# Norm and operand steps issued singly inside the gate's chain of MLP 1's last tile, one PSUM layout for both MLPs, and two norms in MLP 2's second group

## The chip, the cores and the metric

One NeuronCore of one Trainium2 chip runs the whole program. The metric is device microseconds of one execution, lower is better. Matrix products run on TensorE (PE in the profile, its weight loads PEld), element-wise work on VectorE (DVE), ScalarE (ACT) and GpSimd (POOL); SyncE (SP) issues the DMAs. The change leaves every result as it is and moves work in time and between engines.

## What is computed

Retention attention over 4 x 576 tokens with 8 heads of 64, then a first MLP with a gate h * cos(h), then an RMS norm and a gated second MLP, all in fp32. The change touches what follows the attention:

```python
x = _moe_ref(x=x, **moe_kwargs)          # MLP 1, 2304 tokens, 512 -> 2048 -> 512
    h = x @ w_in
    g = h * np.cos(h)
    return g @ w_out
return _moe2_ref(x=x, **moe2_kwargs)     # norm and MLP 2, 512 -> 1536 -> 512
    rms = np.sqrt(np.mean(x * x, axis=-1, keepdims=True) + 1e-06)
    xn = x / rms * rms_g
    g = xn @ w_gate
    silu = g * (1.0 / (1.0 + np.exp(-g)))
    val = xn @ w_val
    return silu * val @ w_out
```

fp32 accuracy comes from splitting each operand into a high and a low part (a cast, then a subtraction) and adding three products.

## The kernel before, in words

**MLP 1** takes the tokens in five tiles, `ORDER_A = [0, 1, 2, 4, 3]`: tiles 0, 1, 2 and 3 have 512 tokens, tile 4 has 256 and comes fourth. Each tile has 16 slices of the hidden dimension, so there are 80 steps; step i is tile i // 16, slice i % 16. The loop at L592 runs 83 times, because the second product of a step comes `LAG = 3` steps after its first. One step of the loop issues, in this order:

- `hidden` (L373): 12 matmuls of the step's hidden slice into a PSUM tile of `ps_tile` (tag g, three buffers before the change);
- on the last slice of a tile, `split_x` (L164): four casts on ScalarE and four subtractions on VectorE that make the next tile's operands;
- `gate_cos` (L379), called the chain here: a scaled copy to integers on ScalarE (L388), a reduction on VectorE (L389), the sine on ScalarE (L391), a product with the hidden slice on VectorE (L395, the last reader of the PSUM tile), the cast of the high part on ScalarE (L397, into one of LAG buffers), and the subtraction for the low part on VectorE or GpSimd (the argument `eng`, line L113). At five places `next(beside)` lets other work in; before the change that is only the conversion of MLP 2's weights, in 36 pieces (`piece_steps`), the last of them in steps 48, 51, 54 and 65 to 67;
- `out_t` of step i - 3 (L572): 12 matmuls into the four accumulators acc0 to acc3. After a tile's last slice the accumulators are copied to `xall` (L585) and the tile's norm is queued;
- `idle` (L362): pops steps of the queued norm from the list `background`. A None ends a step's popping;
- from step 67 on, `ahead(n)` (L551): the operands of MLP 2's first group (seven high and low parts and four differences, into the slots that MLP 1's weights leave) and the first two weight quads.

The norm of a tile (L307) is four squares on ScalarE with sums on VectorE, the sum's high and low part, a product with a matrix of ones on TensorE that gives the mean (L332, L333), a first guess, three Newton iterations of three VectorE steps each, and four scalings of `xall`.

**MLP 2** has three groups of 768 tokens with 12 quads each (n from 0 to 35). A quad (L687) makes seven products in the two PSUM tiles alpha and beta (tag h, two buffers, a pool of its own that opens when MLP 1's closes); between products ScalarE copies partial sums (L710), and VectorE adds, multiplies and subtracts. Eighteen matmuls of the output product (L675) are put into each quad from n = 2 on; `also(where)` lets other steps in at named places (s1, m11, r11, s4, m22, r22, m21, end). Group 2 (tokens 1536 to 2303) uses tiles 3 and 4 of MLP 1; its operands are made from n = 20 on.

**What sets the order.** From step 16 on ScalarE, VectorE and GpSimd run in the order in which the code issues (`manual_schedule`, L636); TensorE does so only in MLP 2. In MLP 1 a planner that runs when the kernel is built, with costs of its own, orders the matmuls on TensorE's queue, in general in the order of the code, but with a later product ahead of one that it takes to be not ready. Each engine's queue is strictly in order on the chip.

## Time and profile before

| | us |
|---|---|
| median of three runs | 942.12 (940.42 to 942.14) |
| profiled execution | 940.8, its span 939.0 |
| attention, and MLP 1's tile 0 beside it, to step 16 | 0 to 174.88 |
| MLP 1, tiles 0 (second half), 1 and 2, to step 48 | to 351.31 |
| MLP 1, tile 4 (256 wide), steps 48 to 63 | 351.31 to 401.46 |
| MLP 1, tile 3, steps 64 to 82 | 401.46 to 509.36 |
| MLP 2, quads 0 to 2 | 509.36 to 542.15 |
| MLP 2, the rest | 542.15 to 939.0 |

The border of two stages is the start of the first matmul of the later one. Of the 939.0 us TensorE is busy for 908.7; its busy rows overlap, so the distance from one matmul's start to the next one's is what is read here, and not their durations.

### The profile page before, as it was taken

The page shows a single profiled execution, that of the slowest core. Times are in us where ns is not written, and L with a number is a line of the kernel's source. Part 1 is how long each engine was busy: PE and PEld are TensorE (multiplying, and loading weights), DVE is VectorE, ACT ScalarE, POOL GpSimd, SP SyncE. Part 2 cuts the span into 40 slices and gives each one's busy share as a digit, 9 for nine tenths or more (in the row PEclk, how much of TensorE's full clock was granted, in tenths as well). Part 3 has the DMA queues.
Part 4 walks back from the last instruction along what each step waited for, and adds up shares of the span by engine and source line. Part 5 has one row for each costly group of instructions (what it writes and reads, how often), then busy time and mean ns, then how long its engine had stood idle before and what let it go on. Part 6 is the DMA issues. An engine that isn't in the chain of part 4 may idle for free.

```text
span 939.0 us, 12936 instructions
## 1 busy us (share of the span) xinstructions
PE 908.7 (97%) x4996; PEld 797.0 (85%) x4996; DVE 612.3 (65%) x991; ACT 462.6 (49%) x815; POOL 62.3 (7%) x58
## 2 busy tenths in 40 slices
PE   8989999999999999989898899999999999999998
PEld 7778888888887889978676899999889999999997
DVE  3999989778888886668765666676355346333332
ACT  4656666576566665564445444444422234323222
POOL 2321100000000001211221000000000000000000
PEclk9999999999999999999999999999999999999999
DMA  8956451135525433102026366667655555755531
GB/s 332 399 186 214 162 229 64 33 112 189 174 76 191 158 128 130 35 12 89 1 101 235 135 236 257 246 234 260 246 202 202 202 202 213 261 205 206 208 142 67
DMA packets 34733, 163.72 MB, mean 174 GB/s; under 512 B 4080, under 2 KB 5232, under 8 KB 23792
## 3 DMA queue, kind: packets, MB, share of 16 engines
q1 hardware_dynamic: 34672, 162.91, 47.7%
q8 instruction: 39, 0.64, 0.3%
q14 instruction: 22, 0.18, 0.1%
HBM read 123.57 MB, written 39.32 MB: 173 GB/s over the span
## 4 chain that ended last, share of the span: by engine, by line
PE 72%; DVE 18%; ACT 5%; issue 3%; DMA 1%; SPq 0%; POOL 0%; ACTq 0%; DVEq 0%; POOLq 0%
PE h L703 26%; PE acc L675 15%; PE g L176 4%; PE g L177 4%; PE g L178 4%; PE acc L177 4%; PE acc L178 4%; PE acc L176 4%; DVE w L113 2%; DVE r L395 2%; DVE r L389 2%; DVE t L131 2%; PE g L270 1%; DVE t L132 1%; ACT r L391 1%
## 5 line engine op out<-in xcount | busy, mean ns | idle before, releaser
L703 PE MATMUL h<-w 128*128 128x384 f32 x1224 | 231.1, 339 | 6.4 <-ACT s L710 3.2
L703 PEld LDWEIGHTS h<-w 128*128 128x128 f32 x1224 | 216.4, 189 | 14.2 <-ACT s L710 5.2
L675 PE MATMUL acc<-w,shi 128*128 128x512 f32 x432 | 134.4, 392 | 0.0
L176 PE MATMUL acc<-ghi,w 128*128 128x512 f32 (+1 forms) x320 | 118.2, 372 | 4.2 <-ACT ghi L397 3.1
L177 PE MATMUL acc<-glo,w 128*128 128x512 f32 (+1 forms) x320 | 118.4, 370 | 2.8 <-POOL glo L113 2.8
L176 PE MATMUL g<-xhi,w 128*128 128x512 f32 (+1 forms) x320 | 120.0, 375 | 0.7 <-ACT w L148 0.7
L178 PE MATMUL g<-xhi,w 128*128 128x512 f32 (+1 forms) x320 | 118.9, 372 | 1.2 <-DVE w L113 1.2
L177 PE MATMUL g<-xlo,w 128*128 128x512 f32 (+1 forms) x320 | 118.9, 372 | 0.0
L178 PE MATMUL acc<-ghi,w 128*128 128x512 f32 (+1 forms) x320 | 118.0, 369 | 0.0
L710 ACT COPY s<-h 128x384 f32<-128x384 f32 x108 | 51.7, 479 | 129.5 <-PE h L703 129.5
L391 ACT ACTIVATE r<-r,half_pi 128x512 f32<-128x512 f32 (+1 forms) x80 | 54.5, 681 | 79.8 <-DVE r L389 79.6
L675 PEld LDWEIGHTS acc<-w,shi 128*128 128x128 f32 x432 | 80.2, 188 | 13.4
L723 DVE TENSOR_TENSOR sg<-s,h 128x384 f32<-128x384 f32 x54 | 29.9, 554 | 93.1 <-PE h L703 52.6
L675 PE MATMUL acc<-w,slo 128*128 128x512 f32 x216 | 85.4, 396 | 0.0
L176 PEld LDWEIGHTS acc<-ghi,w 128*128 128x128 f32 x320 | 60.3, 189 | 15.7 <-ACT ghi L397 4.3
L177 PEld LDWEIGHTS acc<-glo,w 128*128 128x128 f32 x320 | 60.4, 189 | 13.9 <-POOL glo L113 4.3
L397 ACT CAST ghi<-r 128x512 fp32r<-128x512 f32 (+1 forms) x80 | 46.2, 578 | 50.8 <-DVE r L395 47.6
L735 ACT CAST shi<-v 128x384 fp32r<-128x384 f32 x72 | 37.1, 515 | 69.0 <-DVE v L731 68.9
L176 PEld LDWEIGHTS g<-xhi,w 128*128 128x128 f32 x320 | 61.1, 191 | 11.6 <-ACT w L148 0.9
L178 PEld LDWEIGHTS g<-xhi,w 128*128 128x128 f32 x320 | 60.9, 190 | 11.8 <-DVE w L113 1.6
L177 PEld LDWEIGHTS g<-xlo,w 128*128 128x128 f32 x320 | 61.1, 191 | 10.1
L178 PEld LDWEIGHTS acc<-ghi,w 128*128 128x128 f32 x320 | 60.4, 189 | 9.9
(86 smaller groups left out, 1300.0 us busy)
## 6 DMA issues: line engine op xcount, KB each, us to landing
w<-s SPq DMA_DIRECT2D x24, 1024.0 KB, 4.8
raw<-w_dram SPq DMA_DIRECT2D x36, 512.0 KB, 4.0
w<-w SPq DMA_DIRECT2D x18, 1024.0 KB, 5.1
w<-s SPq DMA_DIRECT2D x24, 768.0 KB, 6.3
raw<-w_dram SPq DMA_DIRECT2D x16, 1024.0 KB, 7.4
x<-qkv_dram SPq DMA_DIRECT2D x15, 1024.0 KB, 9.0
s<-w SPq DMA_DIRECT2D x12, 1024.0 KB, 4.8
s<-w SPq DMA_DIRECT2D x12, 768.0 KB, 3.9
```

The source lines that it names most:

```text
L113: eng.tensor_tensor(dst, src, hi.bitcast(F32), op=ALU.subtract)
L131: nc.vector.scalar_tensor_tensor(t, high, -2 ** 30, t, op0=ALU.bitwise_and, op1=ALU.bitwise_or)
L176: nc.tensor.matmul(dst, a[0], b[0], start=start, stop=False)
L177: nc.tensor.matmul(dst, a[0], b[1], start=False, stop=False)
L178: nc.tensor.matmul(dst, a[1], b[0], start=False, stop=stop)
L391: nc.scalar.activation(r, r, AF.Sin, bias=half_pi, scale=1.0)
L397: nc.scalar.copy(hi, r)
L675: nc.tensor.matmul(acc, (hi, hi, lo)[k][:, c], w[:, u, (0, 1, 0)[k], :], start=start and u == 0 and k == 0, stop=stop and u == 1 and k == 2)
L703: nc.tensor.matmul(bank, a[:, wp], xp[:, c], start=start and kc == 0 and n == 0, stop=kc == 1 and n == 2, skip_group_check=True)
L710: nc.scalar.copy(t, alpha)
L723: nc.vector.tensor_tensor(t, s, bank, op=ALU.add)
L735: nc.scalar.copy(hi, t)
```

## The change

- `norm` returns a list of single steps, each with its engine's letter (A, D or P), and the low part of the sum goes to VectorE. A sum's square and add are now two steps. Between low, mean and guess stand two None each.
- Outside the last tile a step of the loop pops up to two norm steps instead of one: `idle()` and then one more if its letter is D in an odd step and A in an even one. In tile 4 popping stops as before once tile 1's norm is done.
- In the last tile (steps 64 to 79), where no weight piece is due, the five places inside the chain each take one step: A between copy and sine, D between reduction and product, A, D and D behind. They come from `ready` (operands and first quads, filled by `ahead`) and else from `background` (tile 2's norm). In steps 80 to 82 six more places follow.
- The chain's last subtraction goes to VectorE in all steps from 48 on.
- PSUM: acc0 to acc3 live in one pool for the whole kernel; from step 8 on the attention's four banks become h (two buffers), acc4 and acc5, and MLP 1's hidden slices and means take these four in turn.
- The norms of tiles 4 and 3 run in MLP 2's second group, at m22 (up to five A or D steps) and end (up to five) of its quads 1 to 10 (n = 13 to 22). The copies of the last tile's accumulators are spread over quads 0 and 1.

Step by step, the lists give this order. Tile 0's norm starts at step 18 as before; its guess and first Newton step come at step 29, two VectorE steps come at steps 31, 33, 35 and 37. Tile 1's guess comes at step 49 and its two-step visits are at steps 49, 51, 53, 55 and 57, its one-step visits at 50, 52, 54 and 56; tile 2's first square follows at 58. Tile 2's low part comes at step 72, its mean at 74, its guess in the chain of step 77, its last eleven VectorE steps in steps 80 to 82. In the second group the half-wide norm of tile 4 is in n = 13 to 15, that of tile 3 in n = 16 to 18.

```diff
-    banks1 = ExitStack()
-    psp = banks1.enter_context(tc.tile_pool(name="psp", bufs=1, space=PSUM, reuse_waits="tile"))
+    psp = pool("psp", 1, space=PSUM)
+    att = ExitStack()
+    psa = att.enter_context(tc.tile_pool(name="psa", bufs=1, space=PSUM, reuse_waits="tile"))
+    late = {}
     dram = pool("dram", 1, space=bass.MemoryType.DRAM)
+    taken = [0]
+    def hidden_tile():
+        return late["psh"].tile([P, 512], F32, tag="h", bufs=2, name="h")
+    def acc_tile(m):
+        return (psp if m < KC else late["psh"]).tile([P, 512], F32, tag=f"acc{m}", name="acc")
     def ps_tile():
-        return psp.tile([P, 512], F32, tag="g", bufs=3, name="g")
-    def acc_tile(m):
-        return psp.tile([P, 512], F32, tag=f"acc{m}", name="acc")
+        if "psh" not in late:
+            return psa.tile([P, 512], F32, tag="g", bufs=3, name="g")
+        taken[0] += 1
+        return hidden_tile() if taken[0] % 2 else acc_tile(KC + taken[0] // 2 % 2)
...
+    ready, background, normal = [], [], []
...
-            if kc == 0:
-                st["s"] = q
-            else:
-                nc.vector.tensor_tensor(st["s"][:, :n], q[:, :n], st["s"][:, :n], op=ALU.add)
-        def total():
-            hi, lo = tmp(F32R), tmp(F32R)
-            s = st["s"][:, :n]
-            nc.scalar.copy(hi[:, :n], s)
-            minus(nc.gpsimd, lo[:, :n], hi[:, :n], s)
-            st["parts"] = hi, lo
+        def add(kc):
+            nc.vector.tensor_tensor(st[0][:, :n], st[kc][:, :n], st[0][:, :n], op=ALU.add)
+        def high():
+            st["parts"] = tmp(F32R), tmp(F32R)
+            nc.scalar.copy(st["parts"][0][:, :n], st[0][:, :n])
+        def low():
+            hi, lo = st["parts"]
+            minus(nc.vector, lo[:, :n], hi[:, :n], st[0][:, :n])
         def mean():
-            st["mean"] = late["mean"]() if "mean" in late else ps_tile()
+            st["mean"] = hidden_tile() if t in ORDER_A[-2:] else ps_tile()
             hi, lo = st["parts"]
             nc.tensor.matmul(st["mean"][:, :n], ones_r, hi[:, :n], start=True, stop=False)
             nc.tensor.matmul(st["mean"][:, :n], ones_r, lo[:, :n], start=False, stop=True)
...
             nc.vector.scalar_tensor_tensor(x(kc), x(kc), rg_sb[:, kc:kc + 1], st["y"],
                                            op0=ALU.mult, op1=ALU.mult)
-        background.extend([lambda kc=kc: square(kc) for kc in range(KC)])
-        background.append(total)
-        background.extend([None, mean, None, guess] if t != ORDER_A[-1] else [None, mean, guess])
-        background.extend([lambda s=s: newton(s) for _ in range(3) for s in range(3)])
-        background.extend([lambda kc=kc: scale(kc) for kc in range(KC)])
-        background.append(lambda: normal.append(t))
-    def idle(count=1):
+        steps = [("A", lambda: square(0))]
+        for kc in range(1, KC):
+            steps += [("A", lambda kc=kc: square(kc)), ("D", lambda kc=kc: add(kc))]
+        steps += [("A", high), ("D", low), None, None, ("P", mean), None, None, ("D", guess)]
+        if t in ORDER_A[-2:]:
+            steps = [step for k, step in enumerate(steps) if step or k == steps.index(None)]
+        steps += [("D", lambda s=s: newton(s)) for _ in range(3) for s in range(3)]
+        steps += [("D", lambda kc=kc: scale(kc)) for kc in range(KC)]
+        steps.append(("D", lambda: normal.append(t)))
+        return steps
+    def idle(count=1, engines="ADP"):
         for _ in range(count):
             if background and not background[0]:
                 background.pop(0)
                 break
-            if background:
-                background.pop(0)()
+            if background and background[0][0] in engines:
+                background.pop(0)[1]()
+    def pull(engine):
+        for steps in (ready, background):
+            if steps and steps[0] and steps[0][0] == engine:
+                steps.pop(0)[1]()
+                return
+    def other_steps():
+        for engine in "ADADD":
+            pull(engine)
+            yield
     g_parts = {}
...
             late["steps"] = operand_steps(0)
-        while late["steps"] and (len(slots) == n or late["steps"][0].__name__ != "high"):
-            late["steps"].pop(0)()
-        if 7 <= n < 11:
+        if n < 7:
+            places.append(slot())
+            ready.append(late["steps"].pop(0))
+            while late["steps"] and late["steps"][0][0] != "A":
+                ready.append(late["steps"].pop(0))
+        elif n < 11:
             slot()
             if n % 2 == 0:
                 a, b = (t.rearrange("p a b c -> p (a b c)") for t in slots[-2:])
                 sides.append((a[:, :6 * 2 * P].rearrange("p (h n c) -> p h n c", h=2, n=3),
                               b.rearrange("p (h n c) -> p h n c", h=2, n=4)))
-                for step in quad_steps(len(sides) - 1).values():
-                    for part in step:
-                        part()
-        elif n >= 11:
+                for steps in quad_steps(len(sides) - 1).values():
+                    ready.extend(steps)
...
             t0 = TILES[t][0]
-            for m in range(KC):
-                nc.scalar.copy(xall[:, m, t0:t0 + n], accs[t][m][:, :n])
-            norm(t)
+            copies = [lambda m=m: nc.scalar.copy(xall[:, m, t0:t0 + n], accs[t][m][:, :n]) for m in range(KC)]
+            if t == ORDER_A[-1]:
+                late["copies"] = copies
+            else:
+                for copy in copies:
+                    copy()
+            if t not in ORDER_A[-2:]:
+                background.extend(norm(t))
...
+            late["psh"] = pool("psh", 1, space=PSUM)
...
-                     nc.vector if i < NF1 or begun(i) is not None else nc.gpsimd,
-                     piece_steps(begun(i), max(valued, default=None)))
+                     nc.vector if i < NF1 or i >= 3 * NF1 or begun(i) is not None else nc.gpsimd,
+                     piece_steps(begun(i), max(valued, default=None)) if begun(i) is not None or valued
+                     else other_steps() if i >= LAST - NF1 else iter(range(5)))
+        elif i >= LAST:
+            for engine in "ADADDD":
+                pull(engine)
         if i >= LAG:
             out_t(*steps[i - LAG])
         if more:
...
+            idle()
+            idle(1, "D" if i % 2 else "A")
+        elif i >= LAST - NF1:
+            idle(1, "P")
         if i >= LAST - NF1 + LAG and len(slots) < NSLOT_A:
             ahead(len(slots))
         if i == MANUAL - 1:
...
+        alpha = hidden_tile()[:, :HALF]
+        beta = hidden_tile()[:, :HALF]
         plain, sums = side(q)
...
-            assert len(normal) == (4, 5)[g]
+            assert len(normal) == (3, 5)[g]
...
+        if n < 2:
+            for where in ("s4", "end"):
+                more[where] = more.get(where, []) + [("A", late["copies"].pop(0))]
+        if n == NQUAD:
+            background.extend(norm(ORDER_A[-2]) + norm(ORDER_A[-1]))
         if g == 1 and 0 < q < NQUAD - 1:
-            more["end"] = more.get("end", []) + [lambda: idle(4)]
+            more["m22"] = more.get("m22", []) + [("D", lambda: idle(5, "AD"))]
+            more["end"] = more.get("end", []) + [("D", lambda: idle(5))]
         quad(g, q, fill, more)
```

## Rows read from the trace of the kernel before

**Rows 1.** Two stretches: us; busy PE, PEld, DVE, ACT, POOL; clock, DMA share, GB/s.
```profile
401.46:509.36 107.90, 98.02 (x426) 78.88 (x425) 76.68 (x115) 53.03 (x90) 21.80 (x16) 0.97 0.24 91
509.36:542.15 32.79, 29.12 (x145) 26.63 (x144) 17.92 (x33) 17.10 (x33) 0.00 (x0) 0.95 0.30 112
```

**Rows 2.** TensorE's waits from 401.46 to 509.36: total us, times, longest us.
```profile
PE g L332 <- ACT nt L325: 3.6, 2, 3.3
PE acc L176 <- ACT ghi L397: 3.1, 2, 1.7
PE acc L177 <- POOL glo L113: 2.8, 4, 0.9
```

**Rows 3.** Timeline of TensorE: first matmuls of steps 37, 47, 53 and 63.
```profile
291.01 0.39 PE L176 MATMUL g<-xhi,w 128*128 128x512 f32 x1
...
345.41 0.39 PE L176 MATMUL g<-xhi,w 128*128 128x512 f32 x1
...
369.78 0.28 PE L176 MATMUL g<-xhi,w 128*128 128x256 f32 x1
...
398.58 0.28 PE L176 MATMUL g<-xhi,w 128*128 128x256 f32 x1
```

**Rows 4.** Timeline of TensorE around steps 66 to 68; in brackets the idle time before.
```profile
417.49 0.79 PE L332 MATMUL g<-nt,ones_r 128*128 128x512 f32 x1 [3.33 <-ACT nt L325]
...
422.39 0.39 PE L176 MATMUL g<-xhi,w 128*128 128x512 f32 x1
...
423.52 0.39 PE L176 MATMUL acc<-ghi,w 128*128 128x512 f32 x1
```

**Rows 5.** Timeline of the other engines: a chain, then VectorE's operand steps, tile 3.
```profile
404.86 0.69 ACT L388 ACTIVATE r<-g,quarter 128x512 int32<-128x512 f32 x1
407.06 0.69 DVE L395 TENSOR_TENSOR r<-g,r 128x512 f32<-128x512 f32 x1 [0.79 <-ACT r L391]
407.84 0.62 ACT L397 CAST ghi<-r 128x512 fp32r<-128x512 f32 x1 [0.81 <-DVE r L395]
...
457.92 1.63 POOL L113 TENSOR_TENSOR glo<-r,ghi 128x512 fp32r<-128x512 f32 x1 [5.22 <-ACT ghi L397]
458.56 1.81 DVE L113 TENSOR_TENSOR w<-xall,w 128x768 fp32r<-128x768 f32 x1 [0.16 <-ACT w L533]
...
465.30 0.95 DVE L113 TENSOR_TENSOR w<-xall,w 128x768 fp32r<-128x768 f32 x1
```

**Rows 6.** Timeline of VectorE in tile 4, and its split for tile 3.
```profile
374.17 0.42 DVE L389 SCALAR_TENSOR_TENSOR r<-r,g 128x256 f32<-128x256 int32 x1 [0.30 <-ACT r L388]
375.16 0.42 DVE L395 TENSOR_TENSOR r<-g,r 128x256 f32<-128x256 f32 x1 [0.58 <-ACT r L391]
...
376.49 0.42 DVE L389 SCALAR_TENSOR_TENSOR r<-r,g 128x256 f32<-128x256 int32 x1 [0.30 <-ACT r L388]
...
377.86 0.42 DVE L395 TENSOR_TENSOR r<-g,r 128x256 f32<-128x256 f32 x1
378.80 0.43 DVE L113 TENSOR_TENSOR glo<-r,ghi 128x256 fp32r<-128x256 f32 x1 [0.53 <-ACT ghi L397]
379.14 0.69 DVE L131 SCALAR_TENSOR_TENSOR t<-raw,t 128x512 int32<-128x512 int32 x1
...
380.58 0.68 DVE L347 SCALAR_TENSOR_TENSOR nt<-nt 128x512 f32<-128x512 f32 x1
381.18 0.42 DVE L389 SCALAR_TENSOR_TENSOR r<-r,g 128x256 f32<-128x256 int32 x1
...
400.38 2.68 DVE L113 TENSOR_TENSOR xlo<-xall,xhi 128x512 fp32r<-128x512 f32 x4 [0.39 <-ACT xhi L170]
```

**Rows 7.** TensorE's only wait from 131 to 371.
```profile
PE acc L176 <- ACT xall L585: 1.1, 1, 1.1
```

**Rows 8.** Timeline of TensorE in MLP 2's second group: its two longest waits.
```profile
673.25 3.42 PE L703 MATMUL h<-w 128*128 128x384 f32 x18 [1.42 <-ACT s L710]
...
699.36 2.35 PE L703 MATMUL h<-w 128*128 128x384 f32 x12 [0.96 <-DVE sg L723]
```

More of the change, by code (lines that the diff above doesn't have):

```diff
@@ L186, in proj @@
             mm3(dst[:, :n], (whi[:, c], wlo[:, c]), (xhi[:, :n], xlo[:, :n]), kc == 0, kc == KC - 1)
-    att = ExitStack()
     ap = att.enter_context(tc.tile_pool(name="ap", bufs=2, reuse_waits="tile"))
@@ L251, in values @@
             if c == 0:
-                total[0] = psp.tile([P, NPAIR, P], F32, tag="st", name="total")
+                total[0] = psa.tile([P, NPAIR, P], F32, tag="st", name="total")
             for p in range(NPAIR):
@@ L301, in body @@
     nc.sync.dma_start(rg_sb, rg)
-    background, normal = [], []
-    late = {}
+    ready, background, normal = [], [], []
     def norm(t):
@@ L314, in square @@
         def square(kc):
-            q = tmp()
+            q = st[kc] = tmp()
             nc.scalar.activation(q[:, :n], x(kc), AF.Square)
-            if kc == 0:
-                st["s"] = q
-            else:
-                nc.vector.tensor_tensor(st["s"][:, :n], q[:, :n], st["s"][:, :n], op=ALU.add)
-        def total():
-            hi, lo = tmp(F32R), tmp(F32R)
-            s = st["s"][:, :n]
-            nc.scalar.copy(hi[:, :n], s)
-            minus(nc.gpsimd, lo[:, :n], hi[:, :n], s)
-            st["parts"] = hi, lo
+        def add(kc):
[6 more added lines that the diff above has]
+            minus(nc.vector, lo[:, :n], hi[:, :n], st[0][:, :n])
         def mean():
-            st["mean"] = late["mean"]() if "mean" in late else ps_tile()
+            st["mean"] = hidden_tile() if t in ORDER_A[-2:] else ps_tile()
             hi, lo = st["parts"]
@@ L386, in gate_cos @@
         k, r, hi, lo = k[:, :n], r[:, :n], hi[:, :n], lo[:, :n]
-        beside = beside or iter(range(5))
         nc.scalar.activation(k, ps, AF.Identity, bias=quarter, scale=INV_2PI)
@@ L506, in keep @@
                 fetch_values(q + 2)
-        return {"r11": [high0, low0], "m22": [sums0], "r22": [high1], "m21": [low1], "end": [keep]}
+        return {"r11": [("A", high0), ("D", low0)], "m22": [("D", sums0)], "r22": [("A", high1)],
+                "m21": [("D", low1)], "end": [("D", keep)]}
     kept = [[dram.tile([P, 2, n, 2 * P], F32, tag=f"s{n}_{q}", name=f"s{n}_{q}") for n in (3, 4)] for q in range(NQUAD)]
@@ L525, in place @@
         def place(k):
-            t = places.pop(0) if g else slot()
+            t = places.pop(0)
             ops[g, k] = t, t[:, 0, :, :HALF], t[:, 1, :, :HALF]
@@ L537, in low @@
                 minus(nc.vector, lo, hi, src)
-            return [high, low]
+            return [("A", high), ("D", low)]
         def difference(dst, a, b):
-            return [lambda: nc.vector.tensor_tensor(dst, a, b, op=ALU.subtract)]
+            return [("D", lambda: nc.vector.tensor_tensor(dst, a, b, op=ALU.subtract))]
         t1 = difference(x(0, 0), x(0, 1), x(0, 0))
@@ L583, in out_t @@
             t0 = TILES[t][0]
-            for m in range(KC):
-                nc.scalar.copy(xall[:, m, t0:t0 + n], accs[t][m][:, :n])
-            norm(t)
+            copies = [lambda m=m: nc.scalar.copy(xall[:, m, t0:t0 + n], accs[t][m][:, :n]) for m in range(KC)]
+            if t == ORDER_A[-1]:
+                late["copies"] = copies
+            else:
+                for copy in copies:
+                    copy()
+            if t not in ORDER_A[-2:]:
+                background.extend(norm(t))
     steps = [(t, f) for t in ORDER_A for f in range(NF1)]
@@ L624, in body @@
                 converted[0] += 1
-        if i // NF1 != 3 or 1 not in normal:
-            idle(3 if i >= LAST - NF1 else 1)
+        if i < LAST - NF1 and (i // NF1 != 3 or 1 not in normal):
+            idle()
+            idle(1, "D" if i % 2 else "A")
+        elif i >= LAST - NF1:
+            idle(1, "P")
         if i >= LAST - NF1 + LAG and len(slots) < NSLOT_A:
@@ L647, in body @@
     order.enter_context(tc.manual_schedule(engines=ENGINES | {mybir.EngineType.PE}))
-    banks1.close()
-    psp = pool("psp2", 1, space=PSUM)
-    def hidden_tile():
-        return psp.tile([P, 512], F32, tag="h", bufs=2, name="h")[:, :HALF]
-    late["mean"] = lambda: psp.tile([P, 512], F32, tag="h", bufs=2, name="h")
     bx = pool("bx", 2)
@@ L659, in body @@
     gp = pool("gp", 2)
+    assert not ready and not places and not background
     places.extend(bx.tile([P, 2, 2, HALF], F32R, tag="b", name="b") for _ in range(2))
@@ L689, in also @@
         def also(where):
-            for step in more.get(where, ()):
+            for _, step in more.get(where, ()):
                 step()
         val = q % 2
-        alpha = hidden_tile()
-        beta = hidden_tile()
+        alpha = hidden_tile()[:, :HALF]
+        beta = hidden_tile()[:, :HALF]
         plain, sums = side(q)
```

## The prediction

> **What bounds the kernel now.** First the stages, by the first matmul of each: MLP 1's last tile, steps 64 to 82, takes 107.90, TensorE is busy for 98.0 of it and its granted clock is 0.97 [rows 1]. Next, who keeps TensorE waiting there: the high part of a norm's sum (3.6 in two waits), the high part of a gate (3.1), and the low part that GpSimd makes (2.8) [rows 2]; no transfer. So this stage is set by the element-wise chain, the others nearly all by TensorE. Then what the stage would take in full flow. Where nothing waits, step 47 starts 54.40 after step 37, so a step of 24 wide matmuls is 5.44; steps 53 to 63 are 28.80 for ten, 2.88 for a half-wide one [rows 3]. One product is thus 2.72 wide and 1.44 narrow. The stage has 16 wide hidden products (43.5), 3 narrow and 16 wide output products (4.3 + 43.5) and, after the change, one mean of two matmuls (2 x 5.44/24 = 0.45): 91.8. It now takes 16.1 more. The waits named are 9.5 of that; the rest is what comes behind a wait, a pipeline that fills again and a clock that has fallen: 3% of 107.90 is 3.2. The wait of 3.33 before the mean of tile 2 [rows 4] is the longest.
>
> **The last tile: -16.1.** Without guests the chain needs 2.98 from its first copy to the cast (404.86 to 407.84), with ScalarE idle for 0.79 and 0.81 in it, waiting for VectorE [rows 5]. After the change the A steps fall into this idle time, and VectorE has three operations of 0.69 of its own and up to three guests. The widest guest, 768 elements, took 0.95 at 465.30 and 1.81 at 458.56, where GpSimd ran beside it from 457.92 [rows 5]. GpSimd has nothing left from step 48 on, so I take 0.95: 3 x 0.69 + 3 x 0.95 = 4.92 for a step in which TensorE needs 5.44. The chain keeps up, the mean of tile 2 comes two steps behind its low part, and the waits of [rows 2] go: 107.90 becomes 91.8.
>
> The Trainium skill, "SBUF — State Buffer", section "Who interferes with whom", says that a VectorE instruction with two SBUF inputs contends with a GpSimd instruction that reads SBUF. Here the trace agrees, 1.81 against 0.95. By that rule alone the subtraction's move would be a gain in tile 4 too, the term for tile 4 below would be nothing and the sum about -10; the rows of tile 4 speak against it.
>
> **A PSUM slot held by the mean: +2.5.** Slices and means take four slots in turn, so the mean of step 74 has the slot that step 78 wants. It is free when the guess has read it, and the guess is the last guest of chain 77. That chain starts when hidden 77 ends, and takes 2.98 to the cast, 0.62 for it, 0.69 for the subtraction and 0.69 for the guess's first operation: 5.0, and 0.6 more if guests hold it up. TensorE has one output product, 2.72, until it wants the slot: a wait of 2.3 to 2.9. If the planner puts the next output product ahead, the wait is nothing. Bounds 0 and 3.0.
>
> **Tile 4: +4.2.** Its chain now takes 2.32 a step (374.17 to 376.49), under TensorE's 2.88, because VectorE does a norm step while ScalarE casts and GpSimd subtracts [rows 6]. With the subtraction on VectorE the norm steps queue behind it, and the next chain behind them: reduction to product 0.99 (374.17 to 375.16), product to subtraction 0.94 (377.86 to 378.80), 0.34 to what follows (379.14), and 0.60 for each norm step (380.58 to 381.18): 2.27 bare, 2.87 with one, 3.47 with two. Against 2.32 the steps 51 to 57 add 0.60 (second norm step), 0.55, 1.15, 0 (a weight piece, VectorE subtracts there before too), 1.15, 0.55 and 1.15: 5.15. Step 50 adds some 0.5, and tile 2's square on ScalarE at 58 as much: 6.2. Steps 59 to 62 cost the same before and after, so this is not made up in comparison. The split of tile 3 queues behind chain 62 on both engines; its first subtraction ended 0.67 after 400.38, hidden 64 started at 401.46, so 0.4 is spare: hidden 64 starts 5.8 late. Meanwhile TensorE could do two narrow output products, 2.9, if the planner has them ahead; it does such things, since at 422.39 hidden 68 starts before the output product at 423.52 [rows 4]. Bounds 2.9 and 5.8; I take the middle. **Clock: +0.7.** The 3.2 of clock above came in two falls, each behind waits; a gap of this length may bring one, 1.6, or none.
>
> **Accumulator copies: +0.6 and +0.5.** TensorE's only wait in tiles 1 and 2, 1.1, is for the copies at step 34, behind a chain that VectorE delays [rows 7]. One more Newton step (0.60) is ahead of them, at step 33. Bounds 0 and 1.2. At step 66 tile 4's copies come behind a chain that needs more than the 4.16 of a wide and a narrow product. No row shows it; between nothing and twice the row above (2.2), with another hidden product as cover, I take 0.5.
>
> **MLP 2's second group: +1.7.** Two norms in place of most of one. Before, the square, sum and cast at the end of n = 13 made TensorE wait 1.42, and four Newton steps at the end of n = 15 0.96 [rows 8]: of 4 x 0.69 some 1.8 were free. After: half-wide operations at n = 13, -0.4. At n = 15 ten half-wide steps (0.43 each, [rows 6]): five at m22 push VectorE back by about 1.3, five at the end are 2.15: 1.65 beyond the free 1.8, against 0.96: +0.7. At n = 17 guess and three Newton steps, 3.2, are 1.4 beyond it, against 0.2: +1.2. Tile 4's mean, 0.2. Bounds 0 (m22 fits into VectorE's own waits) and 3.
>
> **Quads 0 to 2: 0.** Three squares ahead of the first partial sum go (about -0.5); two accumulator copies stand ahead of the first copy of quads 1 and 2 (up to +0.5 each). The stretch has a clock of 0.95, 5% of 32.79 = 1.6, which may come again or not [rows 1]. Bounds -2 and +1.
>
> **At nothing.** The eleven VectorE steps of steps 80 to 82 (about 0.65 each, 7.2) end some 12.3 after hidden 79, with chain 79 ahead of them; VectorE is wanted in quad 0 after four output products and two quad products, about 13. If that 0.7 is gone, it costs one for one. The DMAs of the first two quads are issued two steps later on SyncE, and are wanted in quad 1, over 12 later. The fourth buffer brings nothing: no wait for a PSUM slot stands in [rows 2, 7]. The attention's banks change hands at step 8, after the last attention read or up to 1 before it. In tiles 1 and 2 the second norm step in odd steps is hidden by the lag of three steps.
>
> **Sum.** -16.1 + 2.5 + 4.2 + 0.7 + 0.6 + 0.5 + 1.7 + 0 = -5.9. The profiled execution, 940.8 with its span of 939.0, becomes 934.9; the median of the runs is 1.3 above it: 942.1 - 5.9 = 936.2.
>
> **The rivals.** (1) The planner hides what it can: the slot wait, the clock's fall and the copies at step 66 are nothing and tile 4 costs 2.9: -16.1 + 2.9 + 0.6 + 1.7 = -10.9, 931.2. For it: the order in [rows 4]. Against it: the same planner put a mean where TensorE waited 3.33. (2) TensorE runs in the code's order, and the upper bounds hold: 3.0 + 5.8 + 1.6 + 0.6 + 2.2 + 1.7 = 14.9, so -1.2 and 940.9, no difference that can be told. For it: the regular 5.44 and 2.88 of [rows 3] are the code's order. (3) Slower: the guests hold up the chain that they sit in. A cast into a slot waits until TensorE has read the weights that lay there, and it now stands ahead of the sine. The spare of a step is 5.44 - 4.92 = 0.52; when A steps wait longer than that, or the 768-wide steps take over 1.12 (at 1.81 a step is 7.5), the waits for gate parts in [rows 2] stay and only the norm's 3.6 with one fall of the clock, 1.6, go: -5.2 + 10.2 of the terms above = +5.0, 947.1. Against it: the slots are filled two steps after their last reader, if TensorE keeps the code's order.
>
> **How the numbers follow.** Forecast 48%, its own range 932.5 to 940; rival 1 24%; rival 2 15%; rival 3 10%; others 3%. The range 930.0 to 942.0 takes in the forecast, most of rival 1 and of rival 2. A measurement of this kernel can tell about 0.2% from no change, 1.9 us. Faster by more: 48 + 24 + a third of rival 2, 77%. Within: 13%. Slower: 10%.
>
> **What would show it.** In the trace after: the stage from the first matmul of step 64 to that of quad 0, near 95 (92 and a wait before hidden 78 of about 2.5); no wait for the sum's high part or for GpSimd; a wait for the split's low part before hidden 64 of 3 to 6, with the reductions of tile 4 about 2.9 and 3.5 apart; a wait of TensorE near 1.7 in n = 16 and 1.4 in n = 18. It is wrong if steps 69 to 79 are further apart than 5.44, or if tile 4's narrow steps stay at 2.88 to the end.

## The result and the profile after

The changed kernel takes 930.97 us (median of five runs, 929.44 to 936.03) against 942.14 of before: a ratio of 0.9894, 95% interval 0.9861 to 0.9927. It is faster by 11.2, where the forecast said 5.9; the time lies within the range of the forecast. The profiled execution took 929.44, the fastest of the five, with a span of 927.7.

Stage by stage, by the same first matmuls as before (step 16, 48, 64, quads 0, 3, 13 and 19):

| stage | before | after | difference | forecast |
|---|---|---|---|---|
| start to step 16 | 174.88 | 173.36 | -1.5 | 0 |
| steps 16 to 47 | 176.43 | 176.41 | 0.0 | +0.6 |
| tile 4, steps 48 to 63 | 50.15 | 56.29 | +6.1 | together -8.2 |
| tile 3, step 64 to quad 0 | 107.90 | 90.43 | -17.5 | |
| quads 0 to 2 | 32.79 | 33.79 | +1.0 | 0 |
| quads 3 to 12 | 115.90 | 115.97 | +0.1 | 0 |
| quads 13 to 18 | 73.21 | 73.56 | +0.4 | +1.7 |
| quad 19 to the end | 207.74 | 207.84 | +0.1 | 0 |

Three stages of the kernel after, as in [rows 1] (us; busy PE, PEld, DVE, ACT, POOL with counts; clock; DMA share, GB/s): tile 4, tile 3, quads 0 to 2.

```profile
349.77:406.06 56.29, 54.15 (x402) 51.13 (x401) 37.35 (x81) 27.89 (x62) 1.30 (x1) 1.00 0.23 71
406.06:496.49 90.43, 90.43 (x408) 74.58 (x406) 67.23 (x107) 50.62 (x83) 0.00 (x0) 1.00 0.27 101
496.49:530.28 33.79, 28.02 (x145) 25.01 (x144) 21.19 (x38) 16.86 (x32) 0.00 (x0) 1.00 0.34 128
```

In the last tile TensorE is busy for 90.43 of 90.43: every wait of [rows 2] is gone from this stretch, and so are the falls of the clock that came behind them. It is even 1.4 shorter than the 91.8 of full flow, one narrow product, because the planner put output products of tile 4 ahead of hidden 64. That border is therefore no fair one, and below the two tiles are read together: 158.05 before, 146.72 after. Where an experiment moves products over the border of quad 0, the stretch is taken to quad 3: 190.84 before, 180.51 after.

How it became so stands in the queues of ScalarE and VectorE in the last tile after (start, duration, engine, line, operation, in brackets the idle time before it and what ended it).

```profile
432.16 0.68 ACT L413 ACTIVATE r<-acc,quarter 128x512 int32<-128x512 f32 x1
432.74 0.82 ACT L559 CAST w<-xall 128x768 fp32r<-128x768 f32 x1
433.61 0.72 ACT L416 ACTIVATE r<-r,half_pi 128x512 f32<-128x512 f32 x1
...
432.90 0.68 DVE L414 SCALAR_TENSOR_TENSOR r<-r,acc 128x512 f32<-128x512 int32 x1
433.60 0.96 DVE L123 TENSOR_TENSOR w<-xall,w 128x768 fp32r<-128x768 f32 x1
434.48 0.68 DVE L420 TENSOR_TENSOR r<-acc,r 128x512 f32<-128x512 f32 x1
```

Between two operations of the chain (L413 to L420) stands one guest on each engine. The 768-wide guest of VectorE takes 0.96, the value that the forecast chose between 0.95 and 1.81 [rows 5]; GpSimd has nothing to do.

Tile 4 pays. VectorE there, as in [rows 6], and then TensorE's waits in this stage, where before it had none.

```profile
372.41 0.41 DVE L414 SCALAR_TENSOR_TENSOR r<-r,h 128x256 f32<-128x256 int32 x1
...
374.35 0.43 DVE L123 TENSOR_TENSOR glo<-r,ghi 128x256 fp32r<-128x256 f32 x1 [0.53 <-ACT ghi L422]
374.69 0.68 DVE L356 SCALAR_TENSOR_TENSOR nt<-nt 128x512 f32<-128x512 f32 x1
375.29 0.41 DVE L414 SCALAR_TENSOR_TENSOR r<-r,acc 128x256 f32<-128x256 int32 x1
...
377.58 0.69 DVE L358 SCALAR_TENSOR_TENSOR nt<-nt 128x512 f32<-128x512 f32 x1
378.30 0.69 DVE L354 TENSOR_TENSOR nt<-nt 128x512 f32<-128x512 f32 x1
378.91 0.42 DVE L414 SCALAR_TENSOR_TENSOR r<-r,h 128x256 f32<-128x256 int32 x1
```

```profile
365.18 0.39 PE L186 MATMUL acc<-ghi,w 128*128 128x256 f32 x1 [0.90 <-ACT xall L612]
...
403.04 0.74 PE L186 MATMUL acc<-ghi,w 128*128 128x256 f32 x4 [0.29 <-ACT ghi L422]
405.36 0.74 PE L186 MATMUL acc<-ghi,w 128*128 128x256 f32 x4 [0.62 <-ACT ghi L422]
```

The norm steps (L354 to L358) now stand behind the subtraction (L123) and ahead of the next reduction (L414). With one norm step between them two reductions are 2.88 apart (372.41 to 375.29), with two 3.62 (375.29 to 378.91); the forecast had 2.87 and 3.47. The wait at 365.18 is new and no step of the forecast has it: it is for the copies of tile 2's accumulators at step 50.

The second price stands in quad 0: TensorE's 2.09 for VectorE, which first had to finish tile 2's norm.

```profile
496.49 3.31 PE L738 MATMUL h<-w 128*128 128x384 f32 x18
501.89 2.36 PE L738 MATMUL h<-w 128*128 128x384 f32 x12 [2.09 <-DVE sg L758]
...
498.63 2.74 DVE L361 SCALAR_TENSOR_TENSOR xall<-xall,rg_sb,nt 128x512 f32<-128x512 f32 x4
501.29 0.55 DVE L758 TENSOR_TENSOR sg<-s,h 128x384 f32<-128x384 f32 x1
```

In MLP 2's second group TensorE waits in three quads, as in [rows 8].

```profile
660.76 3.41 PE L738 MATMUL h<-w 128*128 128x384 f32 x18 [0.72 <-ACT s L745]
686.63 2.35 PE L738 MATMUL h<-w 128*128 128x384 f32 x12 [1.34 <-DVE sg L758]
711.36 2.35 PE L738 MATMUL h<-w 128*128 128x384 f32 x12 [0.74 <-DVE sg L758]
```

### The profile page after: what moved, and what is told of

Its sections match the earlier page's. It is cut to its first block, busy times and chain, and to the rows that moved or that the text cites. A ratio compares the mean times of both kernels' runs of the same rounds, so it can differ in the third digit from the quotient of the medians.

```text
span 927.7 us, 12893 instructions
## 1 busy us (share of the span) xinstructions
PE 900.8 (97%) x4996; PEld 790.4 (85%) x4996; DVE 619.5 (67%) x1022; ACT 461.9 (50%) x815; POOL 28.5 (3%) x27
## 4 chain that ended last, share of the span: by engine, by line
PE 76%; DVE 16%; ACT 5%; issue 2%; DMA 1%; SPq 0%; ACTq 0%; DVEq 0%
PE h L738 27%; PE acc L710 15%; PE acc L186 8%; PE acc L187 7%; PE acc L188 7%; PE h L187 3%; PE h L188 3%; PE h L186 3%; DVE t L141 1%; DVE r L420 1%; DVE t L142 1%; DVE w L123 1%; DVE r L414 1%; DVE s L251 1%; DVE glo L123 1%
## 5 line engine op out<-in xcount | busy, mean ns | idle before, releaser
L123 DVE TENSOR_TENSOR glo<-r,ghi 128x512 fp32r<-128x512 f32 (+1 forms) x78 | 49.8, 639 | 33.2 <-ACT ghi L422 31.3
L765 DVE TENSOR_TENSOR v<-s,h 128x384 f32<-128x384 f32 x54 | 29.8, 552 | 53.5 <-PE h L738 40.9
L123 DVE TENSOR_TENSOR slo<-v,shi 128x384 fp32r<-128x384 f32 x72 | 40.1, 557 | 36.7 <-ACT shi L770 36.7
L738 PE MATMUL h<-b,w 128*128 128x384 f32 x288 | 56.7, 337 | 0.0
L187 PE MATMUL h<-xlo,w 128*128 128x512 f32 (+1 forms) x148 | 54.3, 367 | 0.1
L188 PE MATMUL h<-xhi,w 128*128 128x512 f32 (+1 forms) x148 | 54.2, 366 | 0.0
```

Source lines behind the costliest of these rows:

```text
L123: eng.tensor_tensor(dst, src, hi.bitcast(F32), op=ALU.subtract)
L187: nc.tensor.matmul(dst, a[0], b[1], start=False, stop=False)
L188: nc.tensor.matmul(dst, a[1], b[0], start=False, stop=stop)
L738: nc.tensor.matmul(bank, a[:, wp], xp[:, c], start=start and kc == 0 and n == 0, stop=kc == 1 and n == 2, skip_group_check=True)
L765: nc.vector.tensor_tensor(t, s, bank, op=ALU.add)
```

## The experiments

Three questions: which part brings the gain (the smaller load, the spreading, or the place inside the chain); what tile 4's loss is made of; and where the waits in quad 0 and in group 2 come from. Each ratio is to runs of the kernel before on the same chip, with its 95% interval.

### Which part brings the gain

**Only the subtraction to VectorE**, in the kernel before, from tile 4 on.

```diff
-                     nc.vector if i < NF1 or begun(i) is not None else nc.gpsimd,
+                     nc.vector if i < NF1 or i >= 3 * NF1 or begun(i) is not None else nc.gpsimd,
```

> The kernel before with one part of the change alone, the chain's last subtraction on VectorE in all steps from 48 on. Theory: what held up the last tile was mostly the bursts of norm and operand steps, GpSimd's subtraction only the 2.8 of TensorE's waits for it; and in tile 4 VectorE is now full at 2.87 a step against TensorE's 2.88, so the chain does not catch up there and hidden 64 waits 2 to 3 for the split. Tiles 4 and 3 together stay within 2 of the 158.1 before. Rival: GpSimd is the main cause, with its slower subtraction and the contention: tiles 4 and 3 take 6 or more less.

Measured: 948.83, ratio 1.0068 (1.0048 to 1.0088), slower. Tile 4 takes 53.48, 3.3 more than before; both tiles 165.97, 7.9 more. The waits of TensorE in them (in all, times, longest):

```profile
PE acc L176 <- ACT ghi L397: 7.5, 3, 4.6
PE g L332 <- ACT nt L325: 6.3, 1, 6.3
```

The waits for the gate's low part on GpSimd are gone, those for the two high parts together have more than doubled: with bursts left in VectorE's queue, one more operation in it makes each of them later. Neither the theory nor its rival had this. A part of the 7.9 is TensorE's clock, which fell more often among these waits, to a mean of 0.91 in the last tile against 0.97 in [rows 1]:

```profile
403.81:516.30 112.49, 98.75 (x410) 79.46 (x408) 79.54 (x131) 53.79 (x92) 2.02 (x2) 0.91 0.24 90
```

**Only tile 4's norm to the second group**, in the kernel before, eight steps at the end of each quad.

```diff
...
-            norm(t)
+            if t != ORDER_A[-2]:
+                norm(t)
...
+        if n == NQUAD:
+            norm(ORDER_A[-2])
...
-            more["end"] = more.get("end", []) + [lambda: idle(4)]
+            more["end"] = more.get("end", []) + [lambda: idle(8)]
```

> The kernel before with another part alone: the norm of tile 4 leaves the last tile and runs in MLP 2's second group, at the end of its quads, up to eight steps at a time. Theory: half of the last tile's loss comes from that norm, which stands beside the operand steps from step 72 on: the waits from 460 to 475 go, tiles 4 and 3 together take 6 to 8 less than 158.1, and the second group pays some 5 more, since eight steps in one place hold up the next quad: 939 to 941 in all. Rival: the operand steps alone hold the chain up; tiles 4 and 3 gain no more than 2, and the kernel is slower than before by 3 or more.

Measured: 949.24, ratio 1.0074 (1.005 to 1.0097), slower. The two tiles gain 2.9 (155.19) where 6 to 8 were expected, the wait for the norm of tile 2 is the same 3.33 as in [rows 4], and quads 13 to 18 lose 10.2 (83.43), in these waits and two falls of the clock behind the first two:

```profile
690.35 3.92 PE L704 MATMUL h<-w 128*128 128x384 f32 x12 [3.33 <-DVE v L731]
706.70 3.50 PE L704 MATMUL h<-w 128*128 128x384 f32 x12 [3.01 <-DVE sg L724]
733.48 2.37 PE L704 MATMUL h<-w 128*128 128x384 f32 x12 [1.27 <-DVE sg L724]
```

Up to ten steps in two places of a quad (the kernel after) cost 0.35 there, eight in one place 10.2, the two falls of the clock included. The steps are not quite the same: in the kernel before a square and its sum are one step, and the norm's low part is GpSimd's.

**The changed kernel with nothing spread in the last tile**: three norm steps at the end of a step, and whatever a step has ready in one go.

```diff
-                     else other_steps() if i >= LAST - NF1 else iter(range(5)))
-        elif i >= LAST:
-            for engine in "ADADDD":
-                pull(engine)
+                     else iter(range(5)))
...
-            idle(1, "P")
+            idle(3)
...
+            while ready:
+                ready.pop(0)[1]()
```

> The changed kernel, but in the last tile nothing is spread: the norm takes three steps at the end of each step, and what a step has ready (slices and quads 0 and 1) is issued in one go behind the step's last matmul, as before the change. Theory A (the gain is the spreading): waits for the gate's and the norm's high parts come back in the last tile, which takes 97 to 104 instead of 90.4; step 48 to quad 0 154 to 160, 938 to 944. Theory B (the gain is that the low parts left GpSimd and tile 4's norm the stage): last tile 90 to 92, 931. Neither part alone gained, so a sum between them (934) would say that they work together.

Measured: 939.32, ratio 0.9962 (0.9945 to 0.9978). To quad 0 it is 141.25, which looks like a gain, but the planner had started quad 0 ahead of three output products: to quad 3 it is 188.66, 8.1 more than after and 2.2 less than before. The largest wait, and what VectorE and ScalarE did ahead of it:

```profile
494.56 0.51 PE L737 MATMUL h<-w 128*128 128x384 f32 x2
499.87 0.79 PE L186 MATMUL acc<-ghi,w 128*128 128x512 f32 x1 [4.80 <-ACT ghi L422]
...
494.63 0.43 DVE L515 TENSOR_TENSOR z<-z 128x256 f32<-128x256 f32 x1
...
495.09 1.14 ACT L521 CAST w<-z 128x512 fp32r<-128x512 f32 x2 [2.74 <-DVE z L515]
496.13 0.68 ACT L413 ACTIVATE r<-acc,quarter 128x512 int32<-128x512 f32 x1
```

ScalarE stood for 2.74 at a cast of quad 1's weights that needed VectorE's sums, with the start of chain 78 behind it. The expected length to quad 0 was a miss, the total was met; spreading is worth 8.1 of the 10.3 that the stretch gained. In these 8.1 stands a fall of the clock that began in the wait:

```profile
497.80:504.60 6.80, 4.73 (x10) 3.43 (x11) 3.37 (x5) 3.51 (x6) 0.00 (x0) 0.50 1.01 401
```

**Spread, but behind the chain**: the same five steps per step, pulled after the chain has been issued instead of between its operations.

```diff
-                     else other_steps() if i >= LAST - NF1 else iter(range(5)))
+                     else iter(range(5)))
+            if i >= LAST - NF1 and begun(i) is None and i != LAST - NF1 + 4:
+                for engine in "ADADD":
+                    pull(engine)
```

> The changed kernel, with the same single steps in the last tile in the same steps, but all five behind the chain and none inside it. Theory A: what helps is that each step has few of them and that tile 4's norm is gone, and a lag of three steps covers the rest: steps 69 to 71 become some 6.2 apart on VectorE for three steps, 2.3 in all against a slack of 11, and TensorE does not wait: within 1 of the changed kernel. Theory B: the place inside the chain is what helps, since guests behind it make each step longer than 5.44; the waits for gate parts come back and the stage of tile 3 takes 5 to 10 more.

Measured: 930.04, ratio 0.9867 (0.985 to 0.9884); to quad 3 180.32, against 180.51. That the guests fill the chain's idle time [rows 5] is not what brings the gain; few of them in each step is.

**GpSimd in the last tile again**, VectorE in tile 4 as in the change.

```diff
-                     nc.vector if i < NF1 or i >= 3 * NF1 or begun(i) is not None else nc.gpsimd,
+                     nc.vector if i < NF1 or (i // NF1 == 3) or begun(i) is not None else nc.gpsimd,
```

> The changed kernel, with the chain's last subtraction in the last tile (from step 64, but not in the steps with a weight piece) on GpSimd as before the change. Theory: the slack of three steps covers it, GpSimd's 1.3 to 1.6 instead of 0.69 makes the parts later but not more than 5.44 apart: tiles 4 and 3 together within 1 of 146.7. Rival: beside GpSimd the 768-wide guests take 1.8 instead of 0.95 and a step with three of them 7.5; the waits for gate parts come back, 4 or more.

Measured: 929.72, ratio 0.9869 (0.9848 to 0.989); both tiles 146.60, against 146.72. In the last tile the engine of the subtraction makes no difference, though [rows 2] name GpSimd for 2.8: with only the subtraction moved, above, such waits had come back as waits for the cast. Behind the tile it does make one: to quad 3 it is 179.23, 1.3 less than after, as VectorE, with fewer operations in its queue, is done sooner and the wait of 2.09 in quad 0 shrinks.

```profile
503.96 2.38 PE L738 MATMUL h<-w 128*128 128x384 f32 x12 [0.63 <-DVE sg L758]
```

### What tile 4's loss is made of

**GpSimd in tile 4**, with the change's two norm steps in odd steps.

```diff
-                     nc.vector if i < NF1 or i >= 3 * NF1 or begun(i) is not None else nc.gpsimd,
+                     nc.vector if i < NF1 or i >= LAST - NF1 or begun(i) is not None else nc.gpsimd,
```

> The changed kernel, with the chain's last subtraction in tile 4 (steps 48 to 63) back on GpSimd, on VectorE only from step 64. Theory: tile 4 loses its 4 us because the norm steps queue behind that subtraction (reductions 2.9 to 3.5 apart); with GpSimd a step with two norm steps is 0.99 + 0.34 + 2 x 0.60 = 2.5, under TensorE's 2.88, so the chain of step 62 is over 4 earlier, hidden 64 starts without a wait, and tiles 4 and 3 together take 3 to 4 less than the 146.7 of the changed kernel: 927 for the time. Rival: it is the second norm step in odd steps alone, on whichever engine the subtraction is: no more than 1 less.

Measured: 932.51, ratio 0.9897 (0.9878 to 0.9917). Both tiles 145.95, 0.8 less than after: a miss, as the engine alone is not tile 4's loss. Chain 62's reduction does start 50.3 after hidden 48 instead of 53.6, but then no output product is put ahead of hidden 64 (192 matmuls of output products start in tile 4's stage, 209 after), and TensorE waits for the split of tile 3 that queues behind the chain:

```profile
405.42 0.50 PE L186 MATMUL h<-xhi,w 128*128 128x512 f32 x1 [1.29 <-ACT xhi L180]
406.32 0.51 PE L187 MATMUL h<-xlo,w 128*128 128x512 f32 x1 [0.40 <-DVE xlo L123]
```

**The guess of tile 2 two steps earlier**: no empty steps between its mean and its guess.

```diff
-        steps += [("A", high), ("D", low), None, None, ("P", mean), None, None, ("D", guess)]
+        steps += [("A", high), ("D", low), None, None, ("P", mean)] + ([None, None] if t != ORDER_A[2] else []) + [("D", guess)]
```

> The changed kernel, without the two None between the mean and the guess of tile 2, so that the guess comes in the chain of step 75 and not of step 77. Theory: the wait of 2.09 in quad 0 for VectorE comes from the norm steps left over to steps 80 to 82, and these are late because hidden 78 waits for the PSUM slot of the mean; now step 78 follows step 77 after 5.44, seven steps instead of eleven are left over, and the wait in quad 0 goes: 2 less, 929. Rival: the first quads of MLP 2 wait anyway, for the partial sums and the table of the new activation; quads 0 to 2 stay within 0.5 of the 33.8 of the changed kernel.

Measured: 931.16, ratio 0.9875 (0.9858 to 0.9893). The wait of 2.09 in quad 0 is gone, and hidden 78 starts 5.44 after hidden 77 instead of 8.29. The stage of quads 0 to 2 gained only 1.0 (32.74), as its profile holds a fall of the clock:

```profile
498.97:531.71 32.74, 29.23 (x145) 26.36 (x144) 16.54 (x31) 16.74 (x32) 0.00 (x0) 0.95 0.34 127
519.80:523.20 3.40, 3.34 (x12) 2.83 (x11) 2.25 (x5) 1.38 (x3) 0.00 (x0) 0.50 0.28 113
```

**Both together**, the early guess and GpSimd in tile 4.

> Both edits, the subtraction of tile 4 on GpSimd and the early guess. Theory: the two losses are apart and add: 5 to 6 less than the changed kernel, 925. Rival: one of them only covers the other, 3 less.

Measured: 929.28, ratio 0.9855 (0.9837 to 0.9873); both tiles 145.66, quads 0 to 2 31.65 without a fall. So the late guess cost 33.79 - 31.65 = 2.1, in quad 0; to quad 3 both edits save 3.2 (177.31), where 5 to 6 were expected. The late guess acts in two ways. The mean keeps its PSUM slot, so hidden 78 comes late (at 480.00 in the profile of after, when the guess, 0.69 from 479.25, has read the mean), and VectorE stands idle ahead of chain 78's reduction for 3.47, against 0.91 with the early guess alone (first after, then the early guess):

```profile
483.87 0.69 DVE L414 SCALAR_TENSOR_TENSOR r<-r,acc 128x512 f32<-128x512 int32 x1 [3.47 <-ACT r L413]
```

```profile
483.63 0.69 DVE L414 SCALAR_TENSOR_TENSOR r<-r,acc 128x512 f32<-128x512 int32 x1 [0.91 <-ACT r L413]
```

And four more of the norm's steps are left over for the time behind that chain, some 0.72 each. Either is worth more than the wait of 2.09, and no run separates the two.

**Both, and one norm step a step in tile 4.**

```diff
             idle()
-            idle(1, "D" if i % 2 else "A")
+            if i < 3 * NF1:
+                idle(1, "D" if i % 2 else "A")
```

> The changed kernel with the early guess, the subtraction of tile 4 on GpSimd, and one norm step a step in tile 4 instead of up to two. Theory: the norm steps were the other half of tile 4's loss; the reductions are 2.32 apart again, hidden 64 starts without a wait, and tiles 4 and 3 together come to 143 to 143.5, quads 0 to 2 to 31.7: 926.5 for the time. Rival: hidden 64 waits in any case for the split that stands behind chain 62: 145.5, no gain over the kernel with both edits alone.

Measured: 927.09, ratio 0.9848 (0.9824 to 0.9871). Both tiles 143.04, where full flow by the forecast's unit prices is 141.7: three steps with a narrow and a wide product (4.16 each), thirteen narrow ones (2.88), and the last tile's 91.8. The reductions are now 2.32 to 2.33 apart, under TensorE's 2.88, as before the change in [rows 6]:

```profile
384.46 0.42 DVE L414 SCALAR_TENSOR_TENSOR r<-r,acc 128x256 f32<-128x256 int32 x1 [0.31 <-ACT r L413]
...
386.79 0.42 DVE L414 SCALAR_TENSOR_TENSOR r<-r,h 128x256 f32<-128x256 int32 x1 [0.30 <-ACT r L413]
```

**The early guess and one norm step a step, with the subtraction on VectorE**: the diffs of the early guess and of the one norm step.

> Tile 4 has one norm step a step instead of two, the guess of tile 2 comes early, and the low part is still VectorE's. Theory A (the second norm step and the subtraction each carry about half of tile 4's loss): bare chain 2.27 plus one norm step 0.60 is 2.87 against TensorE's 2.88, so nothing builds up in the steps, only what has built up before; step 48 to quad 0 145 to 146, against 146.45 with two norm steps on VectorE and 143.04 with one norm step and GpSimd. Theory B (only the number of norm steps counts, the engine doesn't): 143 to 143.5 as with GpSimd. Theory C (only the engine counts): 146.5. Quads 0 to 2 31.7, and 1.6 more if the clock falls.

Measured: 930.44, ratio 0.9862 (0.9839 to 0.9884). Both tiles 144.59: both the second norm step and the engine count, the norm step somewhat more than expected. Where no weight piece stands between them, the reductions of steps 52 to 59 are 2.88 to 2.89 apart, TensorE's own period:

```profile
385.37 0.41 DVE L414 SCALAR_TENSOR_TENSOR r<-r,acc 128x256 f32<-128x256 int32 x1
...
388.26 0.41 DVE L414 SCALAR_TENSOR_TENSOR r<-r,h 128x256 f32<-128x256 int32 x1
```

A chain that is late when tile 4 begins stays late; with GpSimd it catches up 0.55 in each step. From 146.45 (two norm steps, VectorE) the second norm step takes 1.9 off, GpSimd 0.8, both 3.4.

**Three PSUM buffers instead of four**, with the early guess.

```diff
-        return hidden_tile() if taken[0] % 2 else acc_tile(KC + taken[0] // 2 % 2)
+        return hidden_tile() if taken[0] % 3 else acc_tile(KC)
```

> The kernel with the early guess, with three PSUM buffers in the rotation of slices and means instead of four. Theory A (the fourth buffer brings nothing, as no wait of the kernel before was for a slot): step 48 to quad 0 146.5 and 931, no difference. Theory B (the mean holds one of three slots from its matmuls until the guess has read it, so that only two are left for hidden products): a wait of 1 to 3 at each of the two means of the last tile, step 48 to quad 0 148 to 152, 933 to 937.

Measured: 932.99, ratio 0.9888 (0.986 to 0.9915), which the times alone can't tell from the 0.9875 with four. The trace can: steps 16 to 47 take 1.7 more (178.04), both tiles 2.3 more (148.79), and TensorE waits in tile 4 for the product on VectorE, the last reader of a slot, for 3.0 and 0.9:

```profile
PE h L186 <- DVE r L420: 3.0, 4, 1.2
...
PE acc L186 <- DVE r L420: 0.9, 2, 0.5
```

From step 16 to quad 0 no wait of before was for a slot, with three buffers; the change makes chains late, and the fourth buffer takes up this lateness. At the means of the last tile, where the expectation that it is needed had put its waits, there is none (90.08).

### The second group

**The fastest so far, with the two norms spread over three places of the quads**, one to five steps at each by a table.

```diff
+SPREAD = {0: {"end": 3}, 1: {"r11": 2, "end": 2}, 2: {"r11": 2, "m22": 1, "end": 5}, 3: {"r11": 1, "m22": 1, "end": 2},
+          4: {"r11": 5, "m22": 5, "end": 5}, 5: {"r11": 1, "m22": 1, "end": 2}, 6: {"r11": 4, "m22": 4, "end": 5}, 7: {"m22": 1}}
...
-            more["m22"] = more.get("m22", []) + [("D", lambda: idle(5, "AD"))]
-            more["end"] = more.get("end", []) + [("D", lambda: idle(5))]
+            for where, count in SPREAD[q].items():
+                more[where] = more.get(where, []) + [("D", lambda count=count, where=where: idle(count, "ADP" if where == "end" else "AD"))]
```

> The fastest so far (early guess, GpSimd in tile 4, one norm step a step there), with the two norms of the second group spread over three places of each quad product by a table instead of five at one and five at another. Theory A (the waits of the group, 0.72, 1.34 and 0.74, come from ten VectorE steps in a row ahead of the quad product's own work): quads 13 to 18 go from 73.57 to 70.5 to 72, 924 to 925.5. Theory B (the work of VectorE in these quads is the bound wherever it stands, or the waits are for the norm's own chain): 73.5, 927.

Measured: 923.98 (922.54 to 924.72), ratio 0.9797 (0.9773 to 0.982), the fastest of all. Quads 13 to 18 take 70.45, and TensorE is busy for 70.36 of it:

```profile
404.19:496.71 92.52, 92.26 (x424) 76.71 (x423) 69.24 (x109) 50.65 (x82) 0.74 (x1) 1.00 0.27 99
644.25:714.70 70.45, 70.36 (x365) 64.83 (x364) 40.91 (x78) 26.30 (x56) 0.00 (x0) 1.00 0.61 221
```

All three waits of the group are gone. Its work on VectorE is no bound; where it stands is.

## Why the prediction was right, and short by half

**The last tile, -16.1: right.** 91.8 was forecast without any carry from tile 4. Where tile 4 costs almost nothing, the stage took 92.5 (the early guess with one norm step on GpSimd, and the spread group): 15.4 less than before, and of the missing 0.7 a wait of 0.26 for the accumulator copies at step 66 is one part, which the forecast had at 0.5. The reason given beside it, that guests fit into the chain's idle time, was not the one that counts: behind the chain they cost the same. What the forecast called 4.92 of VectorE in a step of 5.44 leaves room at both places. The forecast also misread one of its rows: the 0.79 of [rows 5] is VectorE's idle time, waiting for the sine, and not ScalarE's; ScalarE's own two there are 0.76 ahead of the sine (at 406.30) and 0.81 ahead of the cast.

**Tile 4, +4.2: right, by the mechanism and nearly the size.** The middle of its bounds, 2.9 and 5.8, is 4.35 and not 4.2. The two tiles' 146.72 less 50.15 for tile 4 before and 91.8 for the last tile is 4.8, where tile 4 and the copies at step 66 were forecast at 4.7. Chain 62's reduction starts 53.6 after hidden 48, against 46.6 before, 7.0 later where 6.2 was forecast; the planner gave back part of it with products put ahead, so that no wait of 3 to 6 stands ahead of hidden 64, which was to be the sign, but 0.29 and 0.62 ahead of output products. Taking the second norm step and VectorE's subtraction away is worth 3.4 of 146.45. The forecast missed the wait of 0.90 at step 50 within it: it took the second norm step in tiles 1 and 2 to be hidden by the lag of three steps, which is so for the output products, but the copies at a tile's end come behind the chain too.

**The rule of the Trainium skill, "SBUF — State Buffer", "Who interferes with whom"**, would have made the move of the subtraction a gain in tile 4. The contention is there (with GpSimd kept in tile 4 a scaling took 1.28 at 386.41 beside it, and 0.74 a step later), but with GpSimd in tile 4 the two tiles are still the shorter by 0.8 to 1.6: a queue's order cost more than the contention.

**The PSUM slot, +2.5: no such wait came.** The planner put an output product ahead of hidden 78, which the forecast allowed for as its lower bound of 0, and TensorE did not wait there. But the last chains and the eleven VectorE steps then came late to quad 0: 2.1 there, of which the slot is one of two causes that were not separated. That 2.1 is near 2.5 is chance. The forecast had put these steps at nothing, hidden with 0.7 to spare, and "one for one" beyond it.

**The fourth buffer, at nothing: wrong.** It was judged by the waits of the kernel before, whose chains were less late. With three buffers the two tiles take 2.3 more.

**The clock, +0.7, and quads 0 to 2, 0.** No fall came in the two tiles. In quads 0 to 2 the wait of 2.1 came in and the fall at 530.0 of the profile before stayed out: +1.0.

**Step 34, +0.6: wrong.** The wait for the copies there was 0.8 after and 1.1 before [rows 7].

**The second group, +1.7: too large.** The three waits measured -0.70, +0.38 and +0.57 against before [rows 8] (0.72 - 1.42, 1.34 - 0.96, 0.74 - 0.17); forecast were -0.4, +0.7 and +1.2. Signs and places hold; five steps pushed back at m22 were partly taken up by VectorE's own waits, its lower bound.

**The start, -1.5, is not the change's.** The profile before has a fall of the clock at 59.0 there, that of after none; over all the profiles of this study the stretch from step 0 to 16 takes 141.4 to 145.7, with none, one or two falls in it.

**The sum.** From -5.9 to the profile's -11.3: the slot's 2.5 and the clock's 0.7 did not come in the two tiles (they measured -11.3, not -8.2); group 2 cost 1.35 less, step 34 0.6 less, the start 1.5 less, and quads 0 to 2 1.0 more. So the main mechanisms were right, and the small costs around them were sized too high together: most were taken near the middle of their bounds, the slot's near the top, and came out lower, while the quads 0 to 2 alone went the other way. Rival 1, in which the planner hides what it can, gave 931.2, the time that came; but that it came out so exactly is chance: it is right for the clock and partly for tile 4, right that no wait came ahead of hidden 78, and it lacks the start's 1.5 and the 2.1 in quad 0. Against rival 3: no guest held up the chain, since TensorE waited for nothing in the last tile.

Three things stay open. The late guess acts in the two ways told above. The two single parts cost 7.9 and gain 2.9 in the two tiles, and together without the spreading gain 2.2 (to quad 3); how much of that comes from the new PSUM layout was not tried. And the median's own -11.2 holds a part that is chance, as the runs of after lie 6.6 apart.

## What to carry to other kernels

An engine with room on average still makes TensorE wait when its side work is queued in bursts: here the same steps cost 8.1 less in the last tile when a few went into each step, and in the second group the norms' steps cost 10.2 with up to eight in one place of a quad, 0.35 with up to ten in two places, and nothing (70.45, against 73.21 before) over three. Before moving an operation from one queue to another, write down what stands between it and the next operation of the critical chain in the new queue: the time from one chain to the next (2.32, 2.88 or 3.62 against TensorE's 2.88) tells whether lateness shrinks, stays or grows. Where a few late steps come at the end of a stage, look for them as a wait at the head of the next.

## What the runs showed of the chip

The falls of TensorE's clock are no fixed part of a kernel's time. Each one in the records is a stretch at 0.50 of full speed, 1.2 instead of 2.4 GHz; most are 3.4 long, some 6.8 (at 497.8 with the bursts), one 10.2 (at 417.5 with only the subtraction moved). The runs of the changed kernel had mean clocks from 0.992 to 1.000 and times from 936.0 to 929.4; 35 runs of the kernel before had 0.984 to 0.995, and the two at these ends 946.0 and 939.5. In the last tile falls stood only in profiles with waits there, among them that of before, at 417.4 and 472.0, at the end of the wait of 3.33 [rows 4] and among the waits for GpSimd of [rows 2], and that of the bursts, from 497.8, within the wait of 4.80. No profile without a wait there had one. In quads 0 to 2 nearly the same waits came with a fall in one kernel (519.8, with the early guess) and without in another (the early guess with GpSimd): 32.74 against 31.65, so a fall cost 1.1 there.
